# Half-head PV moved next to the modulation rows, V's middle third first, and a last output chunk in two pieces instead of three

## The chip, the cores and the metric

The kernel runs on one core of one Trainium2 chip. The metric is the device time in microseconds of that core. Before the change it was 244.3 us, the median of 3 runs (243.81 to 244.73). A profile comes from one execution; its span begins at the first instruction and ends at the last, and is 1.2 to 1.8 us shorter than the time, by an amount that depends on the kernel, as will matter below. The traced execution of the kernel before took 243.62 us and is not one of the three. All executions here were with the full TensorE clock (0.998 or more).

## The reference

A DiT block: 2 sequences of 256 tokens, width 1152, 2 heads of 576, FFN width 4608, all bf16.

```python
mod = (silu(c) @ w_mod).reshape(B, 6, 1, D)
shift_a, scale_a, gate_a, shift_m, scale_m, gate_m = [mod[:, i] for i in range(6)]
h = layernorm(x) * (1 + scale_a) + shift_a
q, k, v = split(h @ wqkv)                       # 2 heads of 576
attn = softmax(q k^T * 576 ** -0.5)
x = x + gate_a * ((attn v) @ wo)
h2 = layernorm(x) * (1 + scale_m) + shift_m
out = x + gate_m * (gelu(h2 @ w_fc1) @ w_fc2)
```

## The kernel before

The kernel describes its work as units, one engine each. A list scheduler inside it orders them from their dependencies (TensorE and SyncE keep program order) and then emits semaphore waits. Every matmul increments TensorE's semaphore. A head is 576 wide, four and a half blocks of 128, so the half blocks of both heads are packed side by side into the 128x128 array (`tile_position`), and the rows of `gate_a` and `shift_m` are computed with 2-column weights, four at a time. The parts that matter:

```python
def v_proj(t, ci):                    # V of token tile t, columns 384*ci to 384*ci+383
    bank = v_banks[v_rr[0] % 3]
    ...
    for kt in range(KT):              # 9 matmuls of 384 columns
        mm(o, HX[:, kt, t * 128:(t + 1) * 128], WV[:, kt, ci * CH:(ci + 1) * CH], kt == 0, kt == KT - 1)
    copy_on("act", V[:, t, ci * CH:(ci + 1) * CH], o, CH, False, ...)

def rows():                           # gate_a and shift_m: 4 column tiles of 32, 72 matmuls of 288 columns
    for kt in range(KT):
        for r in range(2):
            for j in range(4):
                ...
                mm(psum[32 * j:32 * j + 2, bank * 512:bank * 512 + RW], ST[:, kt:18:9], WMODR[:, kt, c0:c0 + RW],
                   kt == 0, kt == KT - 1, tile_position=(0, 32 * j))
    for r, eng in ((0, "act"), (1, "dve")):
        copy_on(eng, ROWS[0:98, ...], ps32(3 + r, 0, RW)[0:98, :], RW, False, ...)
    for j in range(2):                # gate_a's row to DRAM ...
        dma(scratch[0, ...], ROWS[32 * j:32 * j + 2, ...], ..., eng="pool")
    gate_load(0, GA)                  # ... and back, broadcast to 128 partitions

def pv_halves():                      # columns 512 to 639 of V: the half block of each head
    for b in range(2):
        for kjt in range(2):
            for h in range(2):
                base = PVB[b][2] * 512            # banks 6 and 7
                mm(psum[64 * h:64 * h + 64, base:base + 256], V[:, 2 * b + kjt, 512 + 64 * h:576 + 64 * h],
                   PTS[2 * b + h][:, kjt, :], kjt == 0, kjt == 1, tile_position=(0, 64 * h))
    for b, eng in ((0, "dve"), (1, "act")):
        copy_on(eng, OT[:, 4, b * 256:(b + 1) * 256], ps32(PVB[b][2], 0, 256), 256, False, ...)   # OT lies over HX

# wo_tile(t): 3 chunks of 9 matmuls; each chunk's evacuation multiplies by the gate row:
dve(550, lambda e, ...: e.tensor_tensor(out=x1c, in0=o, in1=ga, op=ALU.mult), [o, ga], [x1c], ...)
# then + x on POOL, LayerNorm statistics on DVE, normalisation on ACT, transposes (xn2_T), FC1

# emit(), on SyncE, which issues the output stores:
if ins is last_out:
    for o in outs[:-4]:
        eng_handle.wait_ge(dma_sems[o.dma_sem], o.dma_val)
bi = ins.fn(eng_handle)
...
bi.then_inc(sems[e], 1)               # every instruction, every matmul
```

## Time and profile before

| | before |
|---|---|
| span of the profile | 242.34 us |
| TensorE busy | 238.4 us (98%) |
| changes of the array's packing around rows and half-head PV | 4 |
| gate row lands | 83.23 us |
| last matmul ends | 240.09 us |
| from there to the end of the span | 2.25 us |

TensorE is the bound, so two things are to be read: its own stream (gaps between matmuls, which "busy" hides, because a matmul's modelled duration covers its pipeline), and the tail behind its last matmul. The prediction below shows the views of the first. The tail, from the timeline (start, duration, engine, operation, and the idle time before it), shows the last three pieces of the last chunk, with DVE's multiply (L1284) and add (L1285) for each and the stores on SyncE's queue:

```profile
229.43 11.72 SPq L669 DMA_DIRECT2D out_dram<-arena  x5
...
237.55 0.39 DVE L1284 TENSOR_TENSOR arena<-psum,arena 128x224 f32<-128x224 f32 x1 [2.30 <-PE psum L688]
...
239.08 0.26 DVE L1284 TENSOR_TENSOR arena<-psum,arena 128x96 f32<-128x96 f32 x1 [0.71 <-PE psum L688]
...
240.31 0.22 DVE L1284 TENSOR_TENSOR arena<-psum,arena 128x64 f32<-128x64 f32 x1 [0.68 <-PE psum L688]
240.57 0.22 DVE L1285 TENSOR_TENSOR arena<-arena 128x64 bf16<-128x64 f32 x1
```

The last store is issued 0.03 us after DVE ends and lands 1.41 us later. The smaller the last piece, the less lies behind the last matmul; but every piece is 36 more matmuls, each with a small cost of its own.

### The profile page before, as it was taken

Reading aid. Unit: us, or ns where it says so; the run is one execution under the profiler, and the core shown is the slowest. Engines: PE = TensorE matmul, PEld = TensorE weight load, DVE = VectorE, ACT = ScalarE, POOL = GpSimd, SP = SyncE. Lnnn points to the kernel's source line nnn. Section 1 sums busy time; section 2 is a strip of 40 time slices with the busy share of each in tenths; the row PEclk is TensorE's granted clock in tenths of the full one; section 3 lists DMA queues with packets and bytes.
Section 4 is the critical chain, followed back from the end, with each engine's and each line's share of the span. In section 5 each row is a group of like instructions: output and inputs, shape, how many; then the busy total and the mean of one; then the engine's idle time right before and its main releaser. Section 6 shows DMA issues by size and latency. Waiting matters only on the chain.

```text
span 242.3 us, 4076 instructions
## 1 busy us (share of the span) xinstructions
PE 238.4 (98%) x1763; PEld 147.5 (61%) x1763; DVE 120.3 (50%) x218; ACT 67.0 (28%) x136; POOL 21.2 (9%) x39
## 2 busy tenths in 40 slices
PE   7999999999999999999999999999999999999996
PEld 2698854556667666898444444444566656656676
DVE  3814388696997699789999500000022222111112
ACT  5820350355424107973233322222000000000000
POOL 1400000000021186400000000020000000000000
PEclk9999999999999999999999999999999999999999
DMA  6999999999996999989953498012000000000001
GB/s 241 330 381 392 391 392 391 397 413 405 391 356 196 351 395 391 391 266 394 314 164 82 150 320 313 0 29 72 0 16 19 16 16 19 16 16 16 19 24 27
DMA packets 30140, 51.59 MB, mean 213 GB/s; under 512 B 1703, under 2 KB 15787, under 8 KB 30123
## 3 DMA queue, kind: packets, MB, share of 16 engines
q1 hardware_dynamic: 29680, 50.14, 58.0%
q0 software_dynamic: 416, 1.19, 1.6%
q8 instruction: 14, 0.23, 0.4%
q14 instruction: 3, 0.02, 0.0%
q10 hardware_dynamic: 27, 0.00, 0.0%
HBM read 50.14 MB, written 1.19 MB: 212 GB/s over the span
## 4 chain that ended last, share of the span: by engine, by line
PE 97%; DVE 2%; POOL 0%; issue 0%; ACT 0%; DVEq 0%; POOLq 0%
PE psum L688 95%; PE psum L691 2%; DVE arena L739 1%; DVE arena L760 0%; POOL arena L711 0%; DVE arena L740 0%; DVE arena L1284 0%; DVE arena L1285 0%; POOL arena L710 0%; ACT arena L726 0%; DVE arena L727 0%; DVE arena L732 0%; DVE arena L742 0%; POOL arena L717 0%; POOL arena L715 0%
## 5 line engine op out<-in xcount | busy, mean ns | idle before, releaser
L688 PE MATMUL psum<-arena 128*128 128x384 bf16 (+10 forms) x1674 | 234.9, 306 | 1.6 <-POOL arena L711 1.5
L688 PEld LDWEIGHTS psum<-arena 128*128 128x128 bf16 (+3 forms) x1674 | 142.3, 97 | 90.0 <-issue 3.8
L1079 DVE SCALAR_TENSOR_TENSOR arena<-arena 128x1152 f32<-128x1152 bf16 x32 | 44.7, 1414 | 0.6
L1284 DVE TENSOR_TENSOR arena<-psum,arena 128x384 f32<-128x384 f32 (+3 forms) x14 | 7.0, 501 | 68.0 <-PE psum L688 68.0
L1193 ACT ACTIVATE arena<-psum 128x512 bf16<-128x512 f32 (+1 forms) x44 | 22.4, 520 | 42.7 <-PE psum L688 42.7
L683 ACT ACTIVATE arena<-psum 128x512 bf16<-128x512 f32 (+6 forms) x37 | 19.6, 549 | 39.5 <-PE psum L688 37.1
L685 DVE CAST arena<-psum 128x512 bf16<-128x512 f32 (+3 forms) x13 | 8.2, 641 | 11.4 <-PE psum L688 11.3
L669 POOL DMA_DIRECT2D dit_scratch<-arena x3 | 1.8, 616 | 115.7 <-DVE arena L685 58.9
L1161 POOL TENSOR_TENSOR arena<-arena 128x384 f32<-128x384 f32 x12 | 10.9, 910 | 10.8 <-DVE arena L1160 9.5
L1106 DVE CAST arena<-psum 72x32 bf16<-72x32 f32 x1 | 0.2, 186 | 21.3 <-PE psum L688 21.3
L739 DVE BATCH_NORM_STATS2 arena<-arena 128x6 f32<-128x384 f32 (+1 forms) x18 | 9.5, 552 | 0.1
L1166 ACT ACTIVATE arena<-arena 128x1152 bf16<-128x1152 f32 x4 | 5.3, 1345 | 11.9 <-DVE arena L1165 11.9
L691 PEld LDWEIGHTS psum<-arena 128*128 128x128 bf16 (+1 forms) x89 | 5.8, 98 | 2.5 <-issue 0.8
L1160 DVE TENSOR_TENSOR arena<-psum,arena 128x384 f32<-128x384 f32 x12 | 6.5, 549 | 1.6 <-DMA arena<-dit_scratch 1.6
L1285 DVE TENSOR_TENSOR arena<-arena 128x384 bf16<-128x384 f32 (+3 forms) x14 | 7.0, 501 | 0.5
L691 PE MATMUL psum<-arena 128*128 128x128 bf16 (+1 forms) x89 | 7.1, 219 | 0.1
L1180 DVE TENSOR_SCALAR arena<-psum,arena 128x128 bf16<-128x128 bf16 x20 | 5.4, 341 | 1.9 <-PE psum L691 1.9
L1183 ACT ACTIVATE arena<-psum,arena 128x128 bf16<-128x128 bf16 x16 | 6.0, 456 | 0.9 <-PE psum L688 0.6
L1086 DVE TENSOR_REDUCE arena<-arena 128x36 f32<-128x1152 f32 x4 | 5.4, 1348 | 0.0
L1083 DVE STREAM_TRANSPOSE arena<-arena 128x1152 f32<-128x1152 f32 x4 | 5.4, 1364 | 0.0
L1009 ACT ACTIVATE arena<-psum,arena 128x256 bf16<-128x256 f32 x8 | 3.7, 472 | 1.3 <-PE psum L688 0.9
L743 POOL TENSOR_TENSOR arena<-arena 128x1 f32<-128x1 f32 x6 | 3.6, 596 | 2.0 <-DVE arena L742 2.0
(48 smaller groups left out, 44.9 us busy)
## 6 DMA issues: line engine op xcount, KB each, us to landing
arena<-in_w_fc_dram SPq DMA_DIRECT2D x9, 1152.0 KB, 7.3
arena<-in_w_fc_dram SPq DMA_DIRECT2D x4, 2592.0 KB, 17.2
arena<-in_wqkv_dram SPq DMA_DIRECT2D x18, 288.0 KB, 10.2
arena<-in_w_mod_dram SPq DMA_DIRECT2D x3, 1728.0 KB, 20.2
arena<-in_w_mod_dram SPq DMA_DIRECT2D x3, 864.0 KB, 13.7
arena<-in_w_mod_dram SPq DMA_DIRECT2D x9, 288.0 KB, 10.5
arena<-in_wqkv_dram SPq DMA_DIRECT2D x1, 2592.0 KB, 16.6
arena<-in_wo_dram SPq DMA_DIRECT2D x1, 2592.0 KB, 24.4
```

The source lines that it names most:

```text
L683: act(c_act(n), lambda e: e.activation(out=dst, in_=src, func=ACTF.Copy), [src], [dst], name)
L685: dve(c_dve_psum16(n) if psum16 else c_dve_psum32(n), lambda e: e.tensor_copy(dst, src), [src], [dst], name)
L688: S.instr(lambda e: e.matmul(o, lhsT=l, rhs=r, start=st, stop=sp, **kw), reads=[l, r], writes=[o])
L691: S.instr(lambda e: e.transpose(o, i_, idn), reads=[i_, idn], writes=[o])
L739: dve(550, lambda e, s=s, o=o: e.bn_stats(out=o, in_=s), [s], [o], "bn_%s_%d" % (tag, ci))
L1079: dve(1270, lambda e, w=w, s=s, acc=acc: e.scalar_tensor_tensor(out=acc, in0=w, scalar=s, in1=acc, op0=ALU.mult, op1=ALU.add), [w, s, acc] ...
L1160: dve(550, lambda e, o=o, ga=ga, x1c=x1c: e.tensor_tensor(out=x1c, in0=o, in1=ga, op=ALU.mult), [o, ga], [x1c], "wo_t1_%d_%d" % (t, ci))
L1161: S.op("pool", 930, lambda e, xs=xs, x1c=x1c: e.tensor_tensor(out=x1c, in0=x1c, in1=xs, op=ALU.add), reads=[x1c, xs], writes=[x1c], name=" ...
L1183: act(440, lambda e, o=o, dst=dst, s1=s1, s2=s2: e.activation(out=dst, in_=o, func=ACTF.Identity, scale=s1, bias=s2), [o, s1, s2], [dst], ...
L1193: act(c_act(ntok), lambda e: e.activation(out=dst, in_=o, func=ACTF.Gelu_apprx_tanh), [o], [dst], "gelu_%d_%d" % (f, tok0))
L1284: dve(c_dve_psum32(w), lambda e, o=o, gm=gm, t1=t1: e.tensor_tensor(out=t1, in0=o, in1=gm, op=ALU.mult), [o, gm], [t1], "fc2_t1_%d_%d" % ( ...
L1285: dve(c_dve_32(w), lambda e, t1=t1, x1c=x1c, ost=ost: e.tensor_tensor(out=ost, in0=t1, in1=x1c, op=ALU.add), [t1, x1c], [ost], "fc2_out_%d ...
```

## The change

Its intent: enter and leave the packed modes of the array once less, by putting the two packed blocks side by side. For that the half-head PV needs its columns of V early, so V's middle third is computed first for all tiles. The destination of its evacuation is memory that V still reads, so the evacuation stays behind V. Independently, the last chunk is stored in 320 + 64 columns instead of 224 + 96 + 64.

```diff
@@ pv_halves split into matmuls and evacuation
+        def pv_halves_ev():
             for b, eng in ((0, "dve"), (1, "act")):
                 copy_on(eng, OT[:, 4, b * 256:(b + 1) * 256], ps32(PVB[b][2], 0, 256), 256, False, "OT_ev%d_4" % b)
@@ the order (before: tile by tile, thirds 0 1 2; pv_halves ahead of pv)
         proj(WQ, 8, 8, HX, 2)
+        v_proj(0, 1)
+        s_and_softmax(0, 1)
+        v_proj(1, 1)
+        s_and_softmax(1, 1)
+        v_proj(2, 1)
+        pt_transposes(0, 0)
+        v_proj(3, 1)
+        pt_transposes(1, 0)
         v_proj(0, 0)
... (cut: two more transposes and v_proj(1, 0) between them)
         v_proj(2, 0)
+        pv_halves()
         rows()
         wfc1_load(0)
         wfc1_load(1)
+        v_proj(3, 0)
+        v_proj(0, 2)
+        v_proj(1, 2)
+        rows_T()
         v_proj(2, 2)
         v_proj(3, 2)
+        pv_halves_ev()
         wfc1_load(2)
         wfc1_load(3)
...
-        pv_halves()
         for b in range(2):
             for h in range(2):
                 pv(b, h)
@@ last chunk
-                pieces = [(0, CH), (CH, 2 * CH), (2 * CH, 3 * CH - 160), (3 * CH - 160, 3 * CH - 64), (3 * CH - 64, 3 * CH)]
+                pieces = [(0, CH), (CH, 2 * CH), (2 * CH, 3 * CH - 64), (3 * CH - 64, 3 * CH)]
```

More of the change, by code (lines that the diff above doesn't have):

```diff
@@ L1209, in build_kernel @@
         proj(WQ, 8, 8, HX, 2)
-        v_proj(0, 0)
-        s_and_softmax(0, 1)
-        v_proj(0, 1)
-        s_and_softmax(1, 1)
-        v_proj(0, 2)
-        pt_transposes(0, 0)
+        v_proj(0, 1)
[6 more added lines that the diff above has]
+        pt_transposes(1, 0)
+        v_proj(0, 0)
+        pt_transposes(0, 1)
         v_proj(1, 0)
-        pt_transposes(1, 0)
-        v_proj(1, 1)
-        pt_transposes(0, 1)
-        v_proj(1, 2)
         pt_transposes(1, 1)
         v_proj(2, 0)
+        pv_halves()
         rows()
@@ L1225, in build_kernel @@
         wfc1_load(1)
-        v_proj(2, 1)
+        v_proj(3, 0)
+        v_proj(0, 2)
+        v_proj(1, 2)
+        rows_T()
         v_proj(2, 2)
-        v_proj(3, 0)
-        rows_T()
-        v_proj(3, 1)
         v_proj(3, 2)
+        pv_halves_ev()
         wfc1_load(2)
```

## The prediction

> **What bounds the kernel now.** I read the page first (busy shares, then the chain that ended last), then the list of what TensorE waited for, then the weight-load timeline around the two places that the change touches, then the queues of DVE, ACT and POOL between the modulation rows and the first FC1 tiles.
>
> The page and the TensorE waits:
>
> ```profile
> PE 238.4 (98%) x1763; PEld 147.5 (61%) x1763; DVE 120.3 (50%) x218; ACT 67.0 (28%) x136; POOL 21.2 (9%) x39
> PE 97%; DVE 2%; POOL 0%; issue 0%; ACT 0%; DVEq 0%; POOLq 0%
> PE psum L688 <- POOL arena L711: 1.5, 1, 1.5
> ```
>
> TensorE sets the time: it is busy for 98% of the span, 97% of the chain is its own work, and its only wait is 1.5 us at the start. So a gain must shorten TensorE's own stream or the tail behind its last matmul. A busy TensorE hides small losses, however. The weight-load timeline (start, duration, group, idle before) around the modulation rows (weights 128x2) and the half-head PV (weights 128x64) shows them:
>
> ```profile
> 65.57 2.06 PEld L688 LDWEIGHTS psum<-arena 128*2 128x2 bf16 x72 [0.32 <-issue]
> 67.88 1.09 PEld L688 LDWEIGHTS psum<-arena 128*128 128x128 bf16 x8 [0.25 <-issue]
> ...
> 75.55 0.36 PEld L688 LDWEIGHTS psum<-arena 128*64 128x64 bf16 x8 [0.32 <-issue]
> 76.10 0.11 PEld L688 LDWEIGHTS psum<-arena 128*128 128x128 bf16 x2 [0.20 <-issue]
> ```
>
> Entering and leaving each of the two column-packed blocks, the weight loads pause 0.20 to 0.32 us with nothing to wait for. Single matmul starts in the trace give what this costs: from the last 384-wide matmul to the first one of the rows is 256 ns instead of the usual 162, from the last rows group to the next V matmul 219 ns instead of 121; the half-head PV has 256 instead of 162 going in and 205 instead of 108 coming out. That is 0.094, 0.097, 0.094 and 0.097 us: four changes of the array's packing at about 95 ns each.
>
> The next view is about slack. DVE's timeline and its windows table (PE, PEld, DVE, ACT, POOL busy in each stretch), ACT's queue, and the weight loads again:
>
> ```profile
> 83.32 0.56 DVE L1160 TENSOR_TENSOR arena<-psum,arena 128x384 f32<-128x384 f32 x1 [1.56 <-DMA arena<-dit_scratch]
> 83.30:100.70 17.40, 17.40 (x129) 11.69 (x127) 17.09 (x46) 8.03 (x15) 12.43 (x15) 1.00 1.05 387
> 100.63 0.16 DVE L1165 SCALAR_TENSOR_TENSOR arena<-arena 128x1 f32<-128x1 f32 x1
> 100.83 2.59 ACT L1166 ACTIVATE arena<-arena 128x1152 bf16<-128x1152 f32 x2
> 102.22 0.54 PEld L691 LDWEIGHTS psum<-arena 128*128 128x128 bf16 x9
> ```
>
> At 83.32 DVE stops idling because the gate row arrives from its round trip through DRAM. From there to 100.7 DVE is busy 17.09 of 17.40 us, with no idle that is not its own dependency latency; its output at 100.63 to 100.79 starts the normalisation on ACT at 100.83 (1.35 us for the first of the two), and 50 ns after that one ends TensorE loads its output, 60 ns after the load would have been due. So TensorE is not waiting there, but by no margin: what moves the gate row's landing moves TensorE at 102.2. The POOL queue shows how the gate row gets there:
>
> ```profile
> 69.32 1.25 POOL L669 DMA_DIRECT2D dit_scratch<-arena  x2 [58.92 <-DVE arena L685]
> 75.97 1.13 POOL L669 DMA_DIRECT2D arena<-dit_scratch  x2 [5.40 <-DMA dit_scratch<-arena]
> ```
>
> The rows' evacuation ends at 68.8, two small stores go to DRAM at 69.32, land at 75.4, the two broadcast loads are issued at 75.97, and the first lands at 83.23.
>
> **What the Trainium skill says.** "TensorEngine Tiling (Array Packing)", Key Properties: changing the tiling mode, not just the tile, drains TensorE. The trace agrees, at 95 ns for each of four changes. By that wording going from 64-wide column tiles (half-head PV) to 32-wide ones (rows) is a change of mode too; this trace has no such pair side by side. "TensorE: Matmul & The Clock Gate", section "Wait — 56ns, not 53.3ns?": a warm matmul is N/2.4 ns plus about 2.5 ns. The trace agrees: 162.5 ns start to start at 384 columns, 95.8 at 224, 42.5 at 96, 29.2 at 64. The same page, "The cost: per-tile semaphore tail": every matmul that increments a semaphore adds to a serial queue, about 26 ns each. The trace has 34 ns between increments and shows the queue: the rows' last matmul is over at 67.95, its evacuations start at 68.32, and the last 64-wide piece is evacuated 0.22 us after its last matmul's end. "DMA: Bandwidth & Descriptors", "Queues, rings and completion order": each DMA engine takes turns between the rows of queues it has work for. Here the gate loads' packets, issued at 75.97, start only at 80.0, when the FC1 load issued at 74.84 is nearly through (it lands at 80.6).
>
> **The change part by part.** (1) Reordering V's thirds: all twelve V blocks remain, 9 matmuls each at 162.5 ns. Only the V columns that the half-head PV reads (512 to 640, inside the middle third) come first. Cost 0. The packed softmax blocks sit between the same number of V blocks as before.
>
> (2) Half-head PV in front of the rows. Before: four mode changes. After: into 64-wide tiles, from those to 32-wide, out again: three. Saved: 1 x 0.095 = 0.10 us of TensorE; if 64 to 32 were free, 0.19. What it waits for is there: its probabilities' copies come from DVE (62.53 to 62.95) and ACT (64.9), a V block of 1.46 us ahead of its new place near 65.6. Its evacuation must stay behind the last V block because its destination is the buffer V reads from; it holds two PSUM banks (6 and 7) that nothing else uses until the transposes at 93.
>
> (3) What moves: the rows start later by the block in front of them, 0.094 + 0.022 (first pair) + 4 x 0.109 = 0.55 us. Their end, the two stores and the gate loads all follow. The last V block also ends 0.55 us later, which delays the FC1 load (issued when V's weights are read) that the gate loads queue behind. PV then starts 0.10 us earlier than before.
>
> (4) The last chunk: 224 + 96 columns become one 320. Per accumulation step 95.8 + 42.5 = 138.3 ns become 320/2.4 + 2.5 = 135.8; times 36 steps, 0.09 us saved, on the path that sets the end. The 320-wide piece's two DVE operations (estimate from 384 columns at 0.56 and 224 at 0.39: 0.49 each, 1.06 with start-up) fit in the 1.23 us until the 64-wide piece needs DVE. Its store goes out about where the 96-wide store went (239.66), 1.16 us ahead of the last; the full chunks' stores land in 1.63 us, so it should land before the last one, which takes 1.4.
>
> Sum of TensorE savings: 0.10 + 0.09 = 0.19 us.
>
> **The rivals.** A: nothing gets in the way, and the 0.19 us show: 244.1. For it: TensorE had no measurable stall in this stretch. B: the gate row takes the gain back. The rows' end is 0.55 us later; whatever part d of that reaches the landing at 83.23 goes through DVE's full queue and ACT to the load at 102.2, so TensorE ends up later by about d instead of earlier by 0.10. The stores wait for FC1 traffic that thins out at 75, so d may be under 0.55; the FC1 load ahead of the gate loads moves by 0.55 itself. I take d = 0.3 to 0.55: total +0.2 to +0.46, so 244.5 to 244.8. For it: the 1.56 us DVE idle and the 60 ns margin; against it: DMA landings scatter, and an early one would hide it. C: the last store. One store of 224 columns took 3.28 us and one full chunk 3.14 against the usual 1.63, both with one of the 16 engines late; if the 320-wide store meets that, the end moves out by about 0.7 us. Four of 14 stores took over 2 us; I give it one chance in ten. D: DVE's transposes, which now have the half-head's evacuation between them, run into PV's evacuations by about 1 us; the PSUM bank this holds is freed about 0.5 us before it is needed, so 0.
>
> **Range and chances.** A with weight 0.35 (-0.19) and B with 0.65 (+0.35): 244.3 + 0.16, so 244.5. The times of before already spread over 0.9 us, which is more than the whole effect: 243.8 to 245.1 should hold it 8 times in 10. A 2% change is 4.9 us; nothing here is that large in either direction.
>
> **What would show it right or wrong.** Right: three instead of four pauses of about 95 ns; the rows' first matmul 0.55 us later; one 36-step block of 135.8 ns; the gate wait of DVE ending later than 83.32, and a gap in TensorE of up to half a microsecond before the transposes or FC1 tiles between 92 and 103. Wrong: the gate row landing no later, with TensorE 0.1 us ahead at 105 (then A holds, and 244.1); the change of mode between 64 and 32 columns costing nothing; a wait of the half-head PV for V or the probabilities; or a late last store.

## The result

The changed kernel took 244.31 us (median of 6 runs, 243.9 to 244.62) against 244.24 us for the kernel before in the same rounds (6 runs, 243.81 to 244.73). The ratio is 1.0002, with a 95% interval of 0.9988 to 1.0017. A ratio here is the mean time of one kernel's fast runs over that of the other's fast runs of the same rounds, so not quite the ratio of the medians. That is no difference that the clock can show.

The trace shows more than the clock. The weight loads of the changed kernel around the packed blocks:

```profile
65.57 0.36 PEld L688 LDWEIGHTS psum<-arena 128*64 128x64 bf16 x8 [0.32 <-issue]
66.13 2.06 PEld L688 LDWEIGHTS psum<-arena 128*2 128x2 bf16 x72 [0.20 <-issue]
68.44 24.18 PEld L688 LDWEIGHTS psum<-arena 128*128 128x128 bf16 x170 [0.25 <-issue]
```

There are three pauses instead of four. Single matmul starts give 0.095 us into the 64-wide tiles, 0.095 from those to the rows, 0.097 out of the rows. The rows' first matmul starts at 66.13 instead of 65.57, 0.56 us later.

The gate row's way, first POOL's part of the timeline (two stores to DRAM, then the two loads that broadcast the row):

```profile
69.88 1.25 POOL L669 DMA_DIRECT2D dit_scratch<-arena  x2 [58.90 <-DVE arena L685]
75.88 1.13 POOL L669 DMA_DIRECT2D arena<-dit_scratch  x2 [4.74 <-DMA dit_scratch<-arena]
```

Then DVE's part, the multiplies by the gate row (L1162):

```profile
82.78 0.56 DVE L1162 TENSOR_TENSOR arena<-psum,arena 128x384 f32<-128x384 f32 x1 [1.12 <-PE psum L688]
...
98.44 0.56 DVE L1162 TENSOR_TENSOR arena<-psum,arena 128x384 f32<-128x384 f32 x1 [0.22 <-PE psum L688]
```

The stores go out at 69.88 instead of 69.32, but the loads that wait for them start at 75.88 instead of 75.97: the delay is gone by then. The gate row lands at 82.69 instead of 83.23, and DVE starts 0.09 us later, at 82.78. (The view puts that wait down to TensorE; DVE waits there for TensorE and for the load, and 0.09 us after the landing is exactly as in the kernel before.) At 98.44 DVE even waits 0.22 us for TensorE, which it did not before. So there is slack here in this execution, and TensorE has no gap.

The tail of the changed kernel:

```profile
238.89 0.49 DVE L1287 TENSOR_TENSOR arena<-psum,arena 128x320 f32<-128x320 f32 x1 [3.74 <-PE psum L688]
239.41 0.49 DVE L1288 TENSOR_TENSOR arena<-arena 128x320 bf16<-128x320 f32 x1
239.93 1.09 SPq L669 DMA_DIRECT2D out_dram<-arena  x2
240.12 0.23 DVE L1287 TENSOR_TENSOR arena<-psum,arena 128x64 f32<-128x64 f32 x1 [0.21 <-PE psum L688]
240.38 0.23 DVE L1288 TENSOR_TENSOR arena<-arena 128x64 bf16<-128x64 f32 x1
```

DVE's last multiply starts at 240.12 instead of 240.31. The last store, however, is issued at 240.69, 0.09 us after DVE's end, where it was 0.03 before.

To compare executions I cut TensorE's stream at two marks: S, the start of the fourth group of transposes at 12.9 us (a text below calls it the third), and M, the first transpose of the probabilities at 58.7 us. The start of the kernel scatters (S lies between 12.93 and 13.69 in 14 profiles), and what comes after it hardly does:

| profile | S | S to M | M to the last matmul's end | gate row lands, after M | gaps of TensorE for it | rest of the span |
|---|---|---|---|---|---|---|
| before | 12.93 | 45.81 | 181.36 | 24.50 | 0 | 2.25 |
| changed | 12.93 | 45.81 | 181.16 | 23.95 | 0 | 2.25 |

The 2.25 us of the kernel before are more than is usual for it: 0.11 us of them lie between the landing of the last store and the end of the span, where its second profile (`b_again`) has 0.04 and 2.20 us in all. Against that the changed tail is 0.05 us longer.

The gain of 0.20 us in TensorE's stream is there, as summed in the prediction (0.19). Why the clock does not show it is what the experiments ask. It is 0.08% of the time, where one execution differs from the next by 0.3%.

### The profile page after: what moved, and what is told of

Same layout as the page of the kernel before. It is cut to its first block, busy times and chain, and to the rows that moved or that the text cites. A ratio compares the mean times of both kernels' runs of the same rounds, so it can differ in the third digit from the quotient of the medians.

```text
span 242.1 us, 3989 instructions
## 1 busy us (share of the span) xinstructions
PE 237.7 (98%) x1717; PEld 146.1 (60%) x1727; DVE 120.0 (50%) x216; ACT 67.0 (28%) x136; POOL 21.8 (9%) x39
## 4 chain that ended last, share of the span: by engine, by line
PE 96%; DMA 2%; DVE 2%; issue 0%
PE psum L688 93%; PE psum L691 2%; DMA arena<-in_x_dram 2%; DVE arena L739 1%; DVE arena L760 0%; DVE arena L740 0%; DVE arena L1287 0%; DVE arena L1288 0%; DVE arena L742 0%
## 5 line engine op out<-in xcount | busy, mean ns | idle before, releaser
L688 PE MATMUL psum<-arena 128*128 128x384 bf16 (+9 forms) x1628 | 234.3, 309 | 2.0 <-POOL arena L711 1.5
L688 PEld LDWEIGHTS psum<-arena 128*128 128x128 bf16 (+1 forms) x1638 | 140.8, 97 | 91.2 <-issue 3.9
L1287 DVE TENSOR_TENSOR arena<-psum,arena 128x384 f32<-128x384 f32 (+2 forms) x13 | 6.8, 527 | 68.3 <-PE psum L688 68.3
L691 PEld LDWEIGHTS psum<-arena 128*128 128x128 bf16 (+1 forms) x89 | 5.8, 98 | 2.4 <-DMA arena<-in_c_dram 0.8
L1162 DVE TENSOR_TENSOR arena<-psum,arena 128x384 f32<-128x384 f32 x12 | 6.5, 550 | 1.4 <-PE psum L688 1.3
L1288 DVE TENSOR_TENSOR arena<-arena 128x384 bf16<-128x384 f32 (+2 forms) x13 | 6.9, 527 | 0.5
```

Source lines behind the costliest of these rows:

```text
L688: S.instr(lambda e: e.matmul(o, lhsT=l, rhs=r, start=st, stop=sp, **kw), reads=[l, r], writes=[o])
L691: S.instr(lambda e: e.transpose(o, i_, idn), reads=[i_, idn], writes=[o])
L1162: dve(550, lambda e, o=o, ga=ga, x1c=x1c: e.tensor_tensor(out=x1c, in0=o, in1=ga, op=ALU.mult), [o, ga], [x1c], "wo_t1_%d_%d" % (t, ci))
L1287: dve(c_dve_psum32(w), lambda e, o=o, gm=gm, t1=t1: e.tensor_tensor(out=t1, in0=o, in1=gm, op=ALU.mult), [o, gm], [t1], "fc2_t1_%d_%d" % ( ...
L1288: dve(c_dve_32(w), lambda e, t1=t1, x1c=x1c, ost=ost: e.tensor_tensor(out=ost, in0=t1, in1=x1c, op=ALU.add), [t1, x1c], [ost], "fc2_out_%d ...
```

## The experiments

Twelve runs were made, two of them of the unaltered kernels. All gave correct results. They come from four sessions on different chips, each with the kernel before beside the others, so ratios are to be compared and not times. The theories at the outset: N, the two savings are real and only too small for the clock; B, the later rows delay the gate row and so take the gain back.

**Each part alone (`p_pv`, `p_tail`).** The first is the changed kernel with the old `pieces` line, the second the kernel before with the new one.

```diff
-                pieces = [(0, CH), (CH, 2 * CH), (2 * CH, 3 * CH - 64), (3 * CH - 64, 3 * CH)]
+                pieces = [(0, CH), (CH, 2 * CH), (2 * CH, 3 * CH - 160), (3 * CH - 160, 3 * CH - 64), (3 * CH - 64, 3 * CH)]
```

> Only the first part: V's order and the half-head PV ahead of the rows; the last chunk stays in 224 + 96 + 64. Theory N (the savings are real and only too small for the clock): the trace shows three changes of packing at 0.095 us instead of four, TensorE reaches the first output-projection matmul 0.10 us earlier than in the kernel before and keeps that to the end; time 0.9996 of before, not to be told from 1. Theory B (the delayed gate row takes it back): gaps in TensorE's stream between 92 and 103 us, summing to 0.2 to 0.5 us; time 1.001 to 1.002 of before.

Measured: 243.94 us, ratio 0.9994 (0.9982 to 1.0007). From M to the last matmul's end 181.25 us: 0.11 less than before. No gap between 92 and 103 us.

> Only the second part: the last chunk in 320 + 64 instead of 224 + 96 + 64. Theory N: the 36 steps take 135.8 ns instead of 138.3, so TensorE's last matmul is 0.09 to 0.10 us earlier and the span too; time 0.9996 of before, within noise. Rival (the larger late store ends last): the 320-wide store lands after the 64-wide one, the span is up to 0.7 us longer, 1.001 to 1.003 of before.

Measured: 244.23 us, ratio 1.0003 (0.9991 to 1.0016). From M to the last matmul's end 181.27 us: 0.09 less. The 320-wide store landed 0.58 us before the 64-wide one, so the rival of the late store falls. But the last store left 0.083 us after DVE's end, as in the changed kernel, and in the kernel before and in `p_pv` it was 0.027. So 0.055 of the 0.09 us are lost again behind TensorE.

Something else differs, and no view of the span shows it. Every run has its span (to 0.1 us). In the runs of `p_pv` and of the kernel before the time is 1.20 to 1.41 us longer than the span; in those of `p_tail` it is 1.69 to 1.76 us longer. On average 0.42 us are added outside the span, more than the whole change saves in TensorE's stream. The section "Outside the span" below returns to it.

In both, N holds for TensorE's stream: 0.11 and 0.09 add up to the 0.20 of the two together. That they are "only too small for the clock" does not follow, given those 0.42 us.

**The cost of a change of packing, 54 times over (`s_sep`, `s_adj`).** Into the first two token tiles of FC2 go groups of unused matmuls, a 64-column pair and a 32-column quad, apart or side by side:

```diff
                     mm(o, GT[j][:, t * 128:(t + 1) * 128], WFC2[:, j, c0:c1], j == 0, j == JT - 1)
+                    if t < 2 and j % 4 == 1:                      # s_adj: == 3
+                        for h in range(2):
+                            mm(psum[64 * h:64 * h + 64, 6 * 512:6 * 512 + 64], GT[0][:, 0:64], WFC2[:, 0, 0:64], True, True,
+                               tile_position=(0, 64 * h))
+                    if t < 2 and j % 4 == 3:
+                        for h in range(4):
+                            mm(psum[32 * h:32 * h + 32, 7 * 512:7 * 512 + 64], GT[0][:, 0:32], WFC2[:, 0, 0:64], True, True,
+                               tile_position=(0, 32 * h))
```

> The disputed cost by itself, many times over: the kernel before with 54 unused packed groups put into the first two token tiles of FC2, each a pair of 64-column matmuls and, two steps later, a quad of 32-column ones, 64 columns of data each, results never read. Four changes of packing per group. If a change costs 0.095 us and the matmuls some 0.03 us per pair or quad: 54 x (0.38 + 0.06) = 24 us more, a ratio near 1.10. If only the drain of the small matmuls counted, much less.

Measured: 270.97 us, ratio 1.1102, so 26.8 us more (24 were expected).

> The same 54 groups with the quad right behind the pair, as the change puts the rows right behind the half-head PV: three changes of packing per group. Theory N (going from 64 to 32 columns costs the same 0.095 us): 54 x (0.285 + 0.06) = 18.6 us more than before, 5.1 us less than with the groups apart. Rival (64 to 32 is free): 10 us less than with the groups apart. Third possibility, an adjacent pair saves nothing: the same time as apart.

Measured: 265.36 us, ratio 1.0868, so 21.2 us more (18.6 were expected). The difference between apart and adjacent is 5.6 us, or 0.104 us per group: one change of packing, about as the first theory has it (5.1), and not the 10 us that a free change from 64 to 32 columns would give. Single starts in `s_adj`: 0.095 us extra into the 64-wide tiles, 0.12 from 64 to 32, 0.11 out again. After each way out the next matmul is 10 ns late as well (173 ns instead of 162 in both kernels; the prediction did not count it), which is why a change saved is worth 0.104 us here and 0.107 in `p_pv` and not 0.095. The weight loads of the two kernels show it, with three pauses of 0.32 us in the shown 1.3 us of the first against two in 1.2 us of the second (64 and 32 side by side count as one block there):

```profile
170.66 0.26 PEld L688 LDWEIGHTS psum<-arena 128*32 128x32 bf16 x6 [0.32 <-issue]
171.23 0.26 PEld L688 LDWEIGHTS psum<-arena 128*64 128x64 bf16 x4 [0.32 <-issue]
171.81 0.10 PEld L688 LDWEIGHTS psum<-arena 128*32 128x32 bf16 x4 [0.32 <-issue]
```

```profile
170.52 0.73 PEld L688 LDWEIGHTS psum<-arena 128*64 128x64 bf16 x10 [0.32 <-issue]
171.57 0.11 PEld L688 LDWEIGHTS psum<-arena 128*64 128x64 bf16 x2 [0.32 <-issue]
```

**Does the gate row follow the rows (`g_late`), and does its landing matter (`g_free`)?** For the first, half-head PV and rows go two V blocks further back. For the second, the FC1 load that keeps the queues full when the row's stores go out is issued later:

```diff
@@ g_late
         v_proj(2, 0)
+        v_proj(3, 0)
+        v_proj(0, 2)
         pv_halves()
         rows()
         wfc1_load(0)
         wfc1_load(1)
-        v_proj(3, 0)
-        v_proj(0, 2)
         v_proj(1, 2)
-        rows_T()
         v_proj(2, 2)
+        rows_T()
         v_proj(3, 2)
@@ g_free
         wfc1_load(0)
-        wfc1_load(1)
...
         wfc1_load(2)
+        wfc1_load(1)
         wfc1_load(3)
```

> The changed kernel with half-head PV and rows moved two more V blocks back, so the rows end 2.9 us later still. Theory B (whatever delays the rows delays the gate row by as much, and TensorE behind it): the gate row lands near 85.6 instead of 82.7 us, TensorE has gaps of 2 to 2.7 us in total between 92 and 103 us, ratio 1.008 to 1.011. Theory Q (the small stores land when the FC1 load before them is through, at about 75.4 us, whenever they were issued): issued at 72.8, landing at 75.4 to 76.5, gate row at 83 to 84, TensorE's gaps under 1 us, ratio 0.999 to 1.004.

Measured: 244.41 us, ratio 1.0013 (0.9999 to 1.0027). The stores were issued at 73.08, 3.2 us later than in the changed kernel, and landed at 76.13, 0.8 us later than its 75.33; the gate row landed at 83.79, and TensorE had one gap of 0.21 us in front of the transposes at 102.5. POOL's queue:

```profile
73.08 1.25 POOL L669 DMA_DIRECT2D dit_scratch<-arena  x2 [62.28 <-DVE arena L685]
76.68 1.13 POOL L669 DMA_DIRECT2D arena<-dit_scratch  x2 [2.34 <-DMA dit_scratch<-arena]
```

That is theory Q, not B: most of a delay of the rows vanishes, because the stores wait for the FC1 traffic ahead of them in any case. (`g_free`, next, tests the reason.)

> The changed kernel with the second FC1 load issued after the third, so that nothing large is in the queues when the two small stores of the rows go out. Theory Q: the stores, issued at 69.9, land within 2.5 to 3 us, near 72.7, and the gate row by 77 to 80, 3 to 6 us earlier; DVE then no longer waits for it at 82. TensorE had no gap for it before, so the time stays: ratio 0.998 to 1.001. If the gate row had cost time in the unprofiled runs, it would be lower by 0.002 or more and the spread smaller.

Measured: 244.05 us, ratio 1.0000 (0.9986 to 1.0014). With the queues free the stores landed 1.6 to 2.2 us after their issue and the gate row at 76.80, six microseconds earlier. DVE no longer waits for it. POOL's queue, to be set against that of the changed kernel above:

```profile
70.24 1.26 POOL L669 DMA_DIRECT2D dit_scratch<-arena  x2 [59.22 <-DVE arena L685]
73.10 1.13 POOL L669 DMA_DIRECT2D arena<-dit_scratch  x2 [1.61 <-DMA dit_scratch<-arena]
```

TensorE's stream from M to its end is 181.16 us, the same as in the changed kernel's profile. So an early gate row gives nothing where there was no gap. In other executions it seems to give something: the changed kernel itself ran in the same rounds (`a_again`, next) and took 244.22 to 244.75 us, where `g_free` took 244.0 to 244.22, 0.35 us less on average. With 5 and 4 runs, and intervals against the kernel before that overlap, this is a hint that theory B holds in some executions, and no proof.

**The changed kernel again (`a_again`), and the kernel before again (`b_again`).** No edit.

> The changed kernel once more, unaltered. Theory N: TensorE's stretch from the third group of transposes (12.9 us in the first profile) to the end of its last matmul is again 0.19 us shorter than in the kernel before (226.97 against 227.16), wherever its start falls; the start itself scatters by some 0.4 us and sets the span. Ratio 0.998 to 1.001.

Measured: 244.46 us, ratio 1.0014 (1.0001 to 1.0027). So here the changed kernel is slower than the kernel before by a little more than the interval allows for chance. The expectation of 181.16 us from M to the end (226.97 from S) failed: it was 181.41. This execution has the gaps of theory B. The weight loads at the first FC1 tile:

```profile
98.64 0.10 PEld L689 LDWEIGHTS psum<-arena 128*128 128x128 bf16 x1 [0.16 <-DVE arena L1183]
98.90 0.33 PEld L689 LDWEIGHTS psum<-arena 128*128 128x128 bf16 x4 [0.16 <-DVE arena L1183]
```

TensorE waits twice for the transposed tiles that DVE evacuates, 0.22 us in sum, because in this execution the gate row landed at 83.62, 24.77 us after M. The stream is 0.25 us longer for it, which is the whole gain.

> The kernel before against itself: what the comparison makes of no difference at all. Ratio 0.9985 to 1.0015. Its trace shows how often the gate row leaves TensorE a gap in this kernel too: landing near 83.2 us none, landing later than 83.4 (for a start of 12.9) a gap of 0.1 to 0.4 us.

Measured: 244.08 us, ratio 0.9995 (0.9979 to 1.0012): what no difference looks like here. From M to the end 181.36 us again, the landing 23.67 us after M, no gap. The landing was not late, so what the expectation says of late ones was not tested.

Put together, the landing after M was 24.50, 24.16, 23.67, 24.39 and 24.63 us in the five profiles with the old order (before, `p_tail`, `b_again`, `s_sep`, `s_adj`; no gap) and 23.95, 23.60, 23.21 and 24.77 in the four with the new order and its FC1 loads untouched (the changed kernel, `p_pv`, `t_wait` below, `a_again`; a gap of 0.22 in the last). It scatters over more than a microsecond, is no later with the new order although the rows are 0.56 us later, and in `a_again` and `t_sem` (below) it costs TensorE what it exceeds about 24.55 by. This is no fixed limit: `g_late`, with 24.91, had a gap of 0.21.

**Fewer semaphore increments (`t_sem`).** The rows' and the last piece's evacuations start well after their last matmul's end. The trace has 34.2 ns between TensorE's increments there, more than the 29.2 ns between 64-wide matmuls. This variant counts only matmuls that something waits for, 141 instead of 1725:

```diff
+        pos = {ins.gidx: i for i, ins in enumerate(ins for u in order["pe"] for ins in u.instrs)}
+        counted = set()
+        for ins in self.instrs:
+            counted.add(max((pos[d.gidx] for d in ins.deps if d.unit.eng == "pe"), default=-1))
+        counted = {g for g, i in pos.items() if i in counted}
... (cut: the values that others wait for count these matmuls only)
-                    else:
+                    elif e != "pe" or ins.gidx in counted:
                         bi.then_inc(sems[e], 1)
```

> The changed kernel, with a semaphore increment only on those matmuls that something waits for (the last of most blocks) instead of on all. If increments are served one every 34 ns, the last 64-wide piece's evacuation starts 0.2 us earlier, and the rows' evacuation 0.37 us earlier: span 0.2 us shorter than the changed kernel's for the same start, ratio 0.998 to 1.000 against before. If the late evacuation has another cause, the 0.22 us between the last matmul's end and DVE stay.

Measured: 244.62 us, ratio 1.0021 (1.0007 to 1.0035): slower than the kernel before by 0.2%, though not to be told from the changed kernel in the same rounds (1.0014). The shorter span that was expected did not come (243.53 us). What was said of the increments was right all the same: DVE's last multiply starts 0.038 us after the last matmul's end, where it was 0.217, and the rows' evacuation 0.05 us after theirs instead of 0.37. S to M is also 0.19 us shorter (45.62), where a gap of 0.12 us near 20 us is gone. Three things in the span cost more than that. The gate row landed 25.02 us after M and TensorE had gaps of 0.46 us. The last store left SyncE 0.62 us after DVE's end. And it landed 2.01 us after its issue, where the last store took 1.40 to 1.42 in every other profile.

```profile
240.36 1.44 SPq L675 DMA_DIRECT2D out_dram<-arena  x2
240.37 0.23 DVE L1293 TENSOR_TENSOR arena<-psum,arena 128x64 f32<-128x64 f32 x1
240.63 0.23 DVE L1294 TENSOR_TENSOR arena<-arena 128x64 bf16<-128x64 f32 x1
```

DVE is done at 240.85, and SyncE issues the last store at 241.47 (the 1.44 us span both stores). In between it works through waits for older stores that landed long ago. The kernel before has ten of them, in five pairs; with one store fewer the changed kernel and this one have nine (the texts below say ten). In the packed trace they follow each other after 0.06 to 0.10 us, but here the last pair comes 0.44 us after the one before it. In the kernel before the waits lie in TensorE's time, between 240.04 and 240.37; in the changed kernel they end at 240.64, just too late.

**The waits moved (`t_wait`).** The changed kernel with those waits one store earlier, where SyncE is idle:

```diff
-                    if ins is last_out:
+                    if ins is outs[-2]:
                         for o in outs[:-4]:
```

> The changed kernel with only SyncE's ten waits moved one store forward. If they held up the last store in it, the store follows DVE's end by 0.03 us instead of 0.08, and the span is 0.05 us shorter; not visible in the time, 0.998 to 1.002.

Measured: 244.39 us, ratio 1.0002 (0.9982 to 1.0022). The last store left 0.029 us after DVE's end and the rest of the span is 2.19 us instead of 2.25, as expected; the clock does not show it.

**Together (`best`), and without the later FC1 load (`t_both`).**

> The changed kernel with three additions: the second FC1 load issued later (gate row early), semaphore increments only where something waits for them, and SyncE's ten waits for older stores moved from in front of the last store to in front of the one before it. If the three costs seen so far are real: TensorE 0.19 us shorter than in the kernel before with no gap between 92 and 103 us, the last evacuation 0.18 us sooner after TensorE's end than in the changed kernel, the last store issued within 0.05 us of DVE's end. Span 0.35 to 0.45 us under the kernel before for the same start, ratio 0.997 to 0.9995. Rival (nothing of this reaches the clock): 1.000 within 0.0015.

Measured: 243.15 us (243.0 to 243.32), ratio 0.9955 (0.9938 to 0.9972). The kernel before is beaten by 1.0 us; that is well clear of its interval. The changed kernel did not run in these rounds, but `t_wait` did, at 244.39. The profile:

| profile | S | S to M | M to the last matmul's end | gate row lands, after M | gaps of TensorE for it | rest of the span |
|---|---|---|---|---|---|---|
| `best` | 13.29 | 45.62 | 181.16 | 17.97 | 0 | 2.00 |
| `t_both` | 13.69 | 45.62 | 181.16 | 22.79 | 0 | 2.00 |
| `t_sem` | 13.04 | 45.62 | 181.67 | 25.02 | 0.46 | 3.20 |
| `a_again` | 13.05 | 45.81 | 181.41 | 24.77 | 0.22 | 2.24 |

> The best kernel without its later FC1 load: the changed kernel with the fewer increments and the ten waits moved. If the gate row's landing is what held back the kernel with fewer increments alone, TensorE again shows gaps of 0.2 to 0.5 us between 92 and 103 us, because it now comes there 0.18 us earlier against the same landing; the tail keeps its 0.25 us; ratio 0.997 to 0.9995, 0.3 to 0.6 us slower than the best kernel. Rival (the later FC1 load gave nothing): no gap, and the same 0.9955 as the best kernel.

Measured: 243.42 us (243.2 to 243.87), ratio 0.9966 (0.9947 to 0.9984). The gate row came early in its profile, so there was no gap to see, and that part of the expectation is not tested. The runs of `best` lie within 0.32 us, those of `t_both` within 0.67, as if some of them had gaps; the intervals of the two overlap, so what the later FC1 load gives is not shown.

Against the kernel before, S to the end of the span is 229.42 us there and 228.78 in `best`: 0.19 from fewer increments before M, 0.20 from the change, 0.25 in the tail, 0.64 in sum (0.59 against `b_again`, with its usual tail). The measured 1.0 us is more, and it is a difference of the spans (241.9 us on average against 242.9). What the remaining 0.4 us are is open: gaps for the gate row in untraced runs of the kernel before would fit its spread in those rounds (243.58 to 245.04), but no profile of it shows one.

**Outside the span.** The time less the span:

| kernels | runs | time less span |
|---|---|---|
| before (all sessions of the experiments), `b_again`, `p_pv`, `s_sep`, `s_adj` | 62 | 1.20 to 1.45 us |
| changed, `a_again`, `p_tail`, `g_late`, `g_free`, `t_wait` | 29 | 1.68 to 1.81 us |
| `t_sem`, `best`, `t_both` | 17 | 1.20 to 1.32 us |

The packed traces hold semaphore events from behind the last instruction. The first of them comes 0.12 to 0.16 us after the end of the span in the first and third rows, and 0.61 to 0.62 us after it in the second. So the new last chunk, with every matmul incrementing, adds 0.4 to 0.5 us after the last instruction, and fewer increments take them away. In `t_sem` 0.44 us stand in front of the last store instead (above), perhaps the same pause at another place. What the pause is, no run shows.

## Why the prediction was right or wrong

The range held the time (244.31 in 243.8 to 245.1), and the 0.2 us that were forecast are less than this comparison resolves. That is partly luck: the range is several times as wide as the effect, and the prediction reached its small sum by a loss (the late gate row) that the traced run does not have, and left out one (outside the span) that all its runs have. Its steps fared differently.

- **The savings in TensorE's stream: right.** 0.10 + 0.09 were predicted; 0.11 + 0.09 were measured apart, 0.20 together. A change from 64 to 32 columns costs what the others do: 0.095 us in the changed kernel, and 0.104 us less per group over 54 groups when one change is saved.
- **The rows 0.55 us later: right (0.56), and the step after it wrong.** The prediction took 0.3 to 0.55 us of it to reach the gate row's landing. About nothing did: stores issued at 69.3 to 70.4 landed at 75.3 to 75.8 in either order, since the FC1 traffic holds them, and a further delay of 3.2 us in `g_late` moved them by 0.8. The FC1 load that the gate loads queue behind did move by 0.56 us (74.84 to 75.40), as predicted, but the gate loads' first packets only from 80.07 to 80.26.
- **The thin margin: right.** TensorE can be held up by the gate row, and was, at the FC1 tile and at the transposes at 102, where the landing came later than about 24.55 us after M. But it is the scatter of the landing that decides this, not the 0.56 us. The old order showed no gap, with landings up to 24.63 us; the new order reaches the spot 0.1 us earlier, so its margin is that much less. B was given the weight of 0.65 for the wrong reason; the middle of the forecast, 244.5, was 0.2 us too high. How often untraced runs have such gaps is not known (`g_free` against `a_again` is the only hint).
- **The end of the last chunk: two terms missed.** The 0.09 us were counted on the path that sets the end. They are on it, but the store before the last one was to go out near 239.66 and went out at 239.93: DVE takes 1.01 us for the 320 columns from 238.89, close to the 1.06 that the prediction itself had, so the time of the store was the slip. SyncE begins its nine old waits only after that store, 0.75 us instead of 1.16 ahead of the last one, and gives back 0.055 us (`p_tail` against before; `t_wait` removes it). The larger term lies outside the span, the 0.42 us of `p_tail`, which the prediction has no term for and no run was made to explain. The store of 320 columns ending last, rival C, did not happen: it took 1.57 to 1.59 us in all nine profiles that have it. The late stores behind C have a companion that the prediction did not see: in the 14 profiles 31 of the 32 output stores that took over 1.9 us overlap one of the 16 KB instruction fetches (queue 8 in `--dma`), of the other 155 stores three do, at their end. The fetch at 239.4 us, beside the late stores of the kernel before, is missing in all profiles with the new last chunk. That the fetch delays the store is not tested.
- **Rival D: harmless as predicted, though not as described.** The half-head's evacuation of the first sequence only waits for the V blocks of that sequence's tokens, so the scheduler put it at 74.6, before the last V block, and the transposes never met PV's evacuations.

Why no gain shows on the clock: TensorE's stream is 0.20 us shorter, but 0.055 us go in the tail and 0.42 us are added after the end of the span, so even without noise no gain was to be expected; and where the gate row comes late, a gap takes the stream's gain too (`a_again`). The trace of `p_tail` and the table above show both losses; what the 0.42 us are stays open. So does why the changed kernel is not slower by as much: its spans average 242.6 us, while those of the kernel before average 242.8 to 243.0 in the four sessions, a larger difference than the traces explain. Single spans of the kernel before run from 242.3 to 243.7 us, and the interval of `b_again` is 0.33% wide, 0.8 us.

## What to carry to other kernels

When one engine is busy all the time, look for its losses in the starts of single instructions, and compare executions between two marks inside the stream; that resolved 0.1 us here where 6 runs of the whole kernel did not resolve 0.3. Then compare the time with the span as well: 0.42 us that no view of the span shows stood against a gain of 0.20. A delay put in front of a transfer does not arrive behind it if the transfer was waiting for a queue anyway, so ask what the transfer waits for before shifting its landing by the delay. And before shortening the last piece of a chain, look at everything the issuing queue does between the last two items: with the waits there moved and fewer semaphore increments (`t_both`), the kernel was 0.3% faster than the kernel before, where the change alone was not.

## What the Trainium skill lacked or had wrong

- "TensorEngine Tiling (Array Packing)", Key Properties, says that a change of tiling mode drains TensorE, but not what that costs. Here 0.094 to 0.097 us each between long matmuls, also from 64-wide to 32-wide column tiles, and 0.095 to 0.12 with 64-column data; after a way out the next matmul is 10 ns late too.
- "TensorE: Matmul & The Clock Gate", "The cost: per-tile semaphore tail", has about 26 ns per increment and treats it as a matter of tiles. Here the increments are 34.2 ns apart, and ordinary 64-wide matmuls at 29.2 ns outrun them too: 36 of them leave the evacuation 0.217 us behind, and 0.038 us with one increment.
- The same page, "Back-to-back issue gap", gives about 81 ns at 128 columns and 131 ns at 512 as what a stream of weight loads and matmuls sustains. In the kernel before, such a stream, one weight load for each matmul, runs at 56 ns (its transposes) and 216 ns, so the formula that the page calls isolated is the one that holds.
- "DMA: Bandwidth & Descriptors", "Queues, rings and completion order", says that each DMA engine takes turns, packet by packet, between the queues it has work for, but not what that means for a small transfer behind a large one. In the kernel before, the first packet of the two 2 KB stores, issued at 69.32 us, starts at 72.85, while some 340 packets per us of the other queue go through; in `g_free` and `best`, with the FC1 load out of the way, it starts 1.3 us after the issue. Landing took 4.5 to 5.8 us against 1.6 to 2.8. Taking turns alone does not account for that; what holds the packets back is not shown.
- No page that I read has the cost of waits that are already satisfied on SyncE: 0.06 to 0.10 us for each pair of them, 0.33 us for the ten in front of the last store of the kernel before. Once, in `t_sem`, 0.44 us passed before a pair, for a reason that no run shows.
